# Part two's plain queries and keys behind the first quarter of w_in, and its plain values as f32 through SyncE

## The chip, the core and the metric

The kernel runs on one core of a Trainium2 chip. The metric is the time of one execution on the device in microseconds (us), from the first to the last instruction of the core; lower is better. All times below are of this one core.

## What is computed

Attention over 8 batches, 8 heads, 576 positions and 64 columns, then a feed-forward network on its output. Four heads ("plain") look at the last 32 positions, four ("dilated") at every fourth position of the last 128. All inputs and the output are f32.

```python
scores = scale * np.matmul(q, k.transpose(0, 1, 3, 2))
mask_plain = (rel >= 0) & (rel < window)                                            # window 32
mask_dil = (rel >= 0) & (rel < window * dilation) & (rel % dilation == 0)           # dilation 4
attn = softmax(np.where(masks, scores, -1e9))
x = (attn @ v).transpose(0, 2, 1, 3).reshape(B * S, H * D)                          # 4608 x 512
h = np.maximum(x @ w_in, 0.0)                                                       # w_in 512 x 2048
out = h * h @ w_out                                                                 # w_out 2048 x 512
```

## The kernel before

Heads are worked in pairs e: 0 and 1 are the plain pairs, 2 and 3 the dilated ones. A pair fills the 128 partitions, 64 rows of `sides` for each head. For batches 0 and 1 the positions are cut in two parts: part 0 has positions 0 to 255, part 1 has 256 to 575. The attention output goes, transposed, into the ring xT, and the feed-forward network takes it in token tiles: four tiles of 256 tokens at the start, then tiles of 512. A tile has a first stage (L676: w_in times xT into PSUM, then ScalarE's Relu, L687, and VectorE's square, L688, into h2T) and a second (L711: h2T times w_out, then ScalarE's copy, L718, and SyncE's store, L650). The kernel cuts this into groups of matmuls, and between the groups it puts pieces of the next batches' attention.

The order is written out by hand in the string PROGRAM (L21). What stands before its first bar runs first, what stands behind bar n runs after group n. The scheduler is off (`manual_schedule`), so each engine takes its instructions in exactly this order, and waits for what they need. The codes:

- `Lb:...` are loads of batch b. `q001` loads q and k of part 0, pairs 0 and 1 (`load_qk`, L161, one load each for q and k); `q023`, `q101`, `q123` are the like for other parts and pairs. `v0d` and `v1d` load the dilated values (L184), `v1r` the last 64 positions of these (L197), `v1p` the plain values of part 1: four loads (L178), one for each of four heads. `i0` to `i3` load the quarters of w_in (L776), `o0` to `o3` those of w_out (L781). All of these are issued by GpSimd, whose loads turn f32 into bf16 in flight.
- For batch 0: `T` transposes q and k on TensorE (L505), `C` copies the result out of PSUM (L512 to L520; a trailing `a` puts the copy on ScalarE, `v` on VectorE), `B` writes the mask as a bias, `S` are the scores (L557), `E` the exponential (L565, and for part 1 the mask product on VectorE, L568), `P` is probabilities times values (L595), `D` their sums by a matrix of ones (L611), `L` and `X` are logarithm and exponential on ScalarE, which give the reciprocal of the sums (L618, L621), `M` multiplies into xT (L628). The two digits are pair and part.
- `wN` and `WN` are N matmuls of zeros (`turn`, L475) that keep TensorE going; `W2+31` adds them onto the scores of pair 3, part 1.
- `h` casts the plain values of part 0 from a buffer of f32 into vbd, the layout that P takes (L803). This buffer, `plain`, is one of the three output buffers osb, borrowed at the start; SyncE and ScalarE load it (L745, two loads each).
- `u`, `m` build masks, `z`, `y`, `n` clear buffers; codes such as `1q1` are steps of later batches.

GpSimd's loads use eight semaphores in turn, so load number n is issued only once load n - 8 has landed. The profile shows this as a wait of GpSimd for a DMA.

The groups of the first two tiles are in an order of their own (L836): groups 0 and 1 are stage one of tile 0 for the first quarter of w_in, pairs 0, 1 and pairs 2, 3 of xT; groups 2 and 3 take the second quarter; group 4 begins tile 1 with the first quarter and pairs 2, 3; groups 5 and 6 take the third quarter for tile 0; group 7 ends what group 4 began, with pairs 0, 1; then come the rest of stage one of tile 1 and the fourth quarter.

Of the kernel before, what the change touches and what calls it, by code (L numbers as in the profile page):

```python
# [18 lines left out]


PROGRAM = (  # L21
    "L0:q001 L0:q023 L0:q101 L0:q123 L0:v0d L0:i0 L0:v1dr L0:i1 L0:v1p L0:i2 L0:i3 L0:o0 L0:o1 L0:o2 L0:o3 "
    "L1:q00123 z y L1:v0dp L1:q10123 L1:v1dpr w9 T00 C00a T10 C10a B00 B10 W2 S00 E00 B20 W1 S10 E10 u B30 W3 "
    "T20q W6 T20k C20v T30 C30v h W3 S20 E20 W2 S30 E30 T01 C01v T11 C11a P00 P10 D00 D10 L00 T21 C21v T31 "
    "C31v W4 S01 S11 X00 M00 E01 E11 P20 P30 D20 D30 L20 X20 M20 S21 S31 W2+31 E21 E31 | | P21 P31 D21 D31 L21 "
    "X21 M21 L31 X31 M31 | | P01 P11 D01 D11 L01 X01 M01 L11 X11 M11 | | | | | | | | | | | | | m n | | | | | "
    "L2:q00123 L2:q10123 | 1q1 1q3 | 1q2f 1k2f | 1k1a 1v3 | 1a2 | 1v2 1k0a 1q0v | 1o2 | 1a0 1a1 | 1k3 1o0 1o1f "
    "| 1a3 1Q0 | 1K0 1o3 | 1Q1 1K1 | 1Q2 | 1b0 | | 1Q3 1K2 L2:vwpdr L3:q00123 L3:q10123 | L2:x | | 2q0 | | 2k0 "
    "1V2 | 1b2 1p0 | 1b1 1V3 1K3 | | 1p2 1p1f | 2a0 1b3 | 2k1l 2o0 1p3f 2b0 2k1h | 2q1 2k2 L3:x | | 2q2 2p0 "
# [34 lines left out]
def kernel(  # L64
# [9 lines left out]
    nc = tc.nc  # L74
    P = nc.NUM_PARTITIONS
    B, H, S, D = q.shape
    DM, DFF = moe_w_in.shape
    NTOK = B * S
    assert H * D == DM
    bf16 = mybir.dt.bfloat16  # L80
    f32 = mybir.dt.float32
# [5 lines left out]
    NB = S // 64  # L87
# [5 lines left out]
    NT = 512  # L93
# [39 lines left out]
    xT = const.tile([P, KT, RING], bf16, name="xT")  # L133
# [345 lines left out]
    def first_step(code: str):  # L479
# [82 lines left out]
        elif what == "E":  # L562
            ps = first.pop(("S", e, part))
            to = pts[e][:, c : c + ps.shape[1]]
            nc.scalar.activation(to, ps, ACT.Exp, scale=SCALE)  # L565
            if part:
                mask = (mask_d if dil else mask_p)[:, c : c + ps.shape[1]]
                nc.vector.tensor_tensor(out=to, in0=to, in1=mask, op=ALU.mult)  # L568
        elif what == "P":
            if ("P", *pair) not in first:  # L570
                if pair in ((2, 0), (2, 1), (0, 1)):
                    od = ps_o.tile([P, 512], f32, name="po"), ps_d.tile([P, 512], f32, name="pd")
                else:
                    pool, nm = (ps_a, "pa") if part else (ps_f, "pf")
                    od = [pool.tile([P, 512], f32, name=nm) for _ in range(2)]
                first.pop("W", None)
                first["P", *pair] = od
            o, d = [x[:, y0 : y0 + w] for x in first["P", *pair]]
            o3, d3 = byr(o), byr(d)
            pt = pts[e]  # L580
            bl = blocks(0, e, part)
            y, dms = c, []
            for x, (i, r, q0, q1) in enumerate(bl):
                z = (q1 - q0) * (RES if r is None else 1)
                quads = dil and i < 8
                for rows in sides if quads else [slice(0, P)]:
                    if r is None:
                        to, rhs = o3[rows, :, q0 - m0 : q1 - m0], byr(pt[rows, y : y + z])
                    else:
                        to, rhs = o3[rows, r, q0 - m0 : q1 - m0], pt[rows, y : y + z]  # L590
                    if quads:
                        lhs = vds[0][rows, e - NE // 2, i // RES, D * (i % RES) : D * (i % RES) + D]
                    else:
                        lhs = vbd[0][:, e, i, :]
                    nc.tensor.matmul(  # L595
                        to, lhs, rhs, start=(x == 0 and y0 == 0), stop=(x == len(bl) - 1), skip_group_check=True
                    )
                if not dil:
                    dms.append((d3[:, :, q0 - m0 : q1 - m0], byr(pt[:, y : y + z])))
                y += z  # L600
            if dil and part == 0:
                dms.append((d, pt[:, 0:w]))
            elif dil:
                main = byr(pt[:, c : c + 448])
                dms += [(d3, main[:, :, 32:112]), (d3[:, :, 0:32], main[:, :, 0:32]),
                        (d3[:, :, 64:80], byr(pt[:, c + 448 : c + 512]))]
            first["D", e, part] = dms
        elif what == "D":
            dms = first.pop(("D", e, part))
            for x, (dd, rh) in enumerate(dms):  # L610
                nc.tensor.matmul(  # L611
                    dd, ones, rh, start=(x == 0 and y0 == 0), stop=(x == len(dms) - 1), skip_group_check=True
                )
        else:
            n = 512 if part == 0 else w
            if what == "L":
                first["X", e, part] = rec = r_pool.tile([P, 512], f32, name="rec")
                nc.scalar.activation(rec[:, 0:n], first["P", e, part][1][:, 0:n], ACT.Ln)  # L618
            elif what == "X":
                rec = first["X", e, part][:, 0:n]  # L620
                nc.scalar.activation(rec, rec, ACT.Exp, scale=-1.0)  # L621
            else:
                o, rec = first["P", e, part][0][:, 0:n], first.pop(("X", e, part))[:, 0:n]
                to = xT[:, e, RES * m0 : RES * m0 + n]
                if part == 0:
                    to = xT[:, e : e + 2, 0:w]
                    o, rec = [x.rearrange("p (e n) -> p e n", e=2) for x in (o, rec)]
                nc.vector.tensor_tensor(out=to, in0=o, in1=rec, op=ALU.mult)  # L628
# [24 lines left out]
    def ffn_groups(tk0: int, nt: int):  # L653
# [49 lines left out]
        def g2(m, part):  # L703
            last = tk0 + P * (m + 1) == NTOK
            if part == 0 or last and part == 2:
                cur[m] = ps_f.tile([P, DM], f32, name="pf")

            c0, c1 = (DM // 2 * (part // 2), DM // 2 * (part // 2 + 1)) if last else (0, DM)
            f0, f1 = (NF // 2 * (part % 2), NF // 2 * (part % 2 + 1)) if last else (4 * part, 4 * part + 4)
            for f in range(f0, f1):  # L710
                nc.tensor.matmul(  # L711
                    cur[m][:, c0:c1], h2[:, f, P * m : P * m + P], w_out_sb[:, f, c0:c1],
                    start=(f == 0), stop=(f == NF - 1),
                )
            if f1 == NF:
                osb = osb_pool.tile([P, DM], f32, name="osb")
                mid = (c0 + c1) // 2 if last else c1
                nc.scalar.copy(osb[:, c0:mid], cur[m][:, c0:mid])  # L718
                if last:
                    nc.vector.tensor_copy(osb[:, mid:c1], cur[m][:, mid:c1])  # L720
                for x in (c0, DM // 2) if c1 - c0 == DM and tk0 == NTOK - NT else (c0,):
                    store(osb, tk0 + P * m, x, DM // 2 if x < min(c1, DM // 2) and tk0 == NTOK - NT else c1)

        return [lambda i=i: g1(i) for i in range(NF // per)] + [
            lambda m=m, part=part: g2(m, part) for m in range(nt // P) for part in range(4)
# [17 lines left out]
    for e, engine in enumerate((nc.sync, nc.scalar)):  # L743
        for hl, rows in enumerate(sides):
            engine.dma_start(  # L745
                plain[rows, e, :, :], v[0, 2 * e + hl, 0:256, :].rearrange("(i p) d -> p i d", p=64)
            )
    near = mk[:, 0:96].rearrange("p (r m) -> p r m", r=RES)

    def put(dst, src):  # L750
        nc.scalar.copy(dst, src)
# [39 lines left out]
    def run(code):  # L791
        if code == "y":
            for nm in "qk":
                nc.gpsimd.memset(staged(1, nm)[64:80, 0, :, :], 0.0)
                nc.gpsimd.memset(staged(2, nm)[64:80, 0, 0 : H // 2, :], 0.0)
        elif code == "z":
            nc.gpsimd.memset(vbd[1][0:64, :, :, 64:128], 0.0)
            nc.gpsimd.memset(vbd[1][64:128, :, :, 0:64], 0.0)
        elif code in "mu":
            masks(int(code == "u"))  # L800
        elif code == "h":
            for rows in sides:
                nc.vector.tensor_copy(vbd[0][rows, 0:2, 0:4, rows], plain[rows, :, :, :])  # L803
        elif code == "n":
            zero_halves(kbd)
            zero_halves(vbd[0][:, NE // 2 :, 0:8, :])
        elif code[0] in "wW":
            n, _, at = code[1:].partition("+")
            turn(int(n), 512 if code[0] == "w" else 256, [int(x) for x in at])
        elif code[0] in "TCBSEPDXM" or code[0] == "L" and code[2:3] != ":":  # L810
            first_step(code)
        elif code[0] != "L":
            step(int(code[0]), code[1:])
        else:
            b, what, part, which = int(code[1]), code[3], code[4:5], code[5:]
            if what == "q":
                load_qk(b, None if part == "w" else int(part), [int(e) for e in which])
            elif what == "x":
                cross_all(b)
            elif what == "v":  # L820
                load_v(b, [0, 1] if part == "w" else [int(part)], which)
            else:
                (load_w_in if what == "i" else load_w_out)(int(part))
# [67 lines left out]
```

The softmax here doesn't subtract the row's maximum and nothing guards it: scores larger than these inputs give would overflow.

## Time and profile before

The median of three runs is 309.02 us (308.62 to 309.26). The profiled execution spans 309.7 us.

| engine | busy, us | share | instructions |
|---|---|---|---|
| TensorE, matmuls (PE) | 301.4 | 97% | 2562 |
| TensorE, weight loads (PEld) | 186.6 | 60% | 2562 |
| VectorE (DVE) | 196.2 | 63% | 645 |
| ScalarE (ACT) | 198.2 | 64% | 425 |
| GpSimd (POOL) | 93.8 | 30% | 138 |

| stretch, us | what runs | PE busy | DMA moved, GB/s |
|---|---|---|---|
| 0 to 10 | batch 0, part 0 | 8.61 of 10.00 | 122 |
| 10 to 18 | batch 0, parts 0 and 1 | 6.58 of 8.00 | 195 |
| 18 to 26.34 | groups 0 to 4, part 1 | 7.15 of 8.34 | 152 |
| 26.34 to 36 | groups 5 on, stage one | 9.66 of 9.66 | 218 |
| 36 to 53 | stage two, batch 1 | 17.00 of 17.00 | 166 |
| 53 to 79 | batches 1 and 2 | 25.32 of 26.00 | 171 |

The granted TensorE clock is 0.998 of full speed. How to read it: PE's busy time takes in the time that matmuls stand in its pipeline, so a busy PE is not PE at its peak; a gap in it is a true wait, though. The DMA view gives bytes as they are written, so a GpSimd load counts half of what it reads. A landing is the issue's start plus the time "to landing". The DMA queues have the names q0 (GpSimd), q1 (SyncE) and q10 (ScalarE); in this program a packet is one row of a load.

### The profile page before, as it was taken

How to read it: one execution, taken by the hardware profiler on the slowest of the kernel's cores; microseconds unless marked ns; L12 is line 12 of the kernel's file. 1: busy time of each engine (PE TensorE's matmuls, PEld its weight loads, DVE VectorE, ACT ScalarE, POOL GpSimd, SP SyncE). 2: the span in 40 equal slices, each digit the busy share in tenths (PEclk: the TensorE clock that was granted, in tenths of full speed). 3: DMA queues.
4: the chain of work that ended last, by engine and by line, in shares of the span. 5: the costliest groups of instructions: out<-in, count | busy, mean ns of one | idle time of the engine just before them, and what ended most of it. 6: DMA issues, size and time to landing. Idle time of an engine off the chain costs nothing.

```text
span 309.7 us, 6806 instructions
## 1 busy us (share of the span) xinstructions
PE 301.4 (97%) x2562; PEld 186.6 (60%) x2562; DVE 196.2 (63%) x645; ACT 198.2 (64%) x425; POOL 93.8 (30%) x138
## 2 busy tenths in 40 slices
PE   8898999999999999999999999999999999999995
PEld 3578856958855555555599555555555555445544
DVE  1555567888989889975798469946994334104400
ACT  7576748849977967795388547854686456216511
POOL 8489775546317345501551041000000000000000
PEclk9999999999999999999999999999999999999999
DMA  7999999999999979999799976502200210121022
GB/s 103 195 143 212 208 151 172 175 141 186 171 130 174 165 139 182 185 144 155 109 127 134 154 121 93 103 8 61 68 3 0 70 69 0 35 69 34 0 61 77
DMA packets 80288, 35.05 MB, mean 113 GB/s; under 512 B 49920, under 2 KB 75648, under 8 KB 80256
## 3 DMA queue, kind: packets, MB, share of 16 engines
q0 software_dynamic: 46592, 18.23, 52.4%
q1 hardware_dynamic: 32976, 16.06, 28.2%
q10 hardware_dynamic: 688, 0.33, 0.5%
q8 instruction: 20, 0.33, 0.4%
q14 instruction: 12, 0.10, 0.1%
HBM read 36.90 MB, written 9.44 MB: 150 GB/s over the span
## 4 chain that ended last, share of the span: by engine, by line
PE 81%; DMA 9%; ACT 3%; POOL 3%; issue 1%; DVE 1%; POOLq 0%; ACTq 0%
PE pf L711 38%; PE pf L676 35%; DMA w_in<-in_moe_w_in_dram 6%; DMA kb<-in_k_dram 4%; PE po L421 3%; PE pd L423 2%; PE pa L312 2%; PE pa L318 1%; POOL qb L161 1%; ACT h2T L687 1%; POOL kb L161 1%; PE pa L236 1%; ACT pt L322 1%; ACT qT L256 1%; ACT rec L425 0%
## 5 line engine op out<-in xcount | busy, mean ns | idle before, releaser
L676 PE MATMUL pf<-xT,w_in 128*128 128x256 bf16 (+1 forms) x768 | 133.5, 326 | 1.3 <-DMA w_in<-in_moe_w_in_dram 1.2
L711 PE MATMUL pf<-w_out_sb,h2T 128*128 128x512 bf16 (+1 forms) x592 | 134.2, 373 | 0.0
L676 PEld LDWEIGHTS <-w_in 128*128 128x128 bf16 x768 | 82.2, 114 | 36.6 <-DMA w_in<-in_moe_w_in_dram 1.8
L687 ACT ACTIVATE h2T<-pf 128x512 bf16<-128x512 f32 x144 | 83.8, 599 | 25.5 <-PE pf L676 24.8
L711 PEld LDWEIGHTS <-h2T 128*128 128x128 bf16 x592 | 54.3, 98 | 53.5
L688 DVE TENSOR_TENSOR h2T<-h2T 128x512 bf16<-128x512 bf16 x144 | 57.9, 422 | 40.2 <-ACT h2T L687 39.0
L718 ACT COPY osb<-pf 128x512 f32<-128x512 f32 (+1 forms) x37 | 21.0, 566 | 43.8 <-PE pf L711 35.8
L436 DVE TENSOR_TENSOR xT<-po,rec 128x288 bf16<-128x288 f32 (+2 forms) x51 | 23.2, 454 | 30.9 <-ACT rec L426 30.4
L178 POOL DMA_DIRECT2D vbd<-in_v_dram x36 | 25.7, 735 | 42.0 <-PE pd L423 37.2
L425 ACT ACTIVATE rec<-pd 128x288 f32<-128x288 f32 (+2 forms) x51 | 20.9, 411 | 20.4 <-PE pd L423 20.4
L322 ACT ACTIVATE pt<-pa 128x352 bf16<-128x352 f32 (+6 forms) x56 | 27.6, 499 | 7.1 <-PE pa L312 4.2
L426 ACT ACTIVATE rec<-rec 128x288 f32<-128x288 f32 (+2 forms) x56 | 24.8, 444 | 1.8
L421 PEld LDWEIGHTS <-vbd 128*128 128x128 bf16 x286 | 17.1, 97 | 9.4 <-issue 0.4
L256 DVE COPY qT<-xx 64x288 bf16<-64x288 bf16 x84 | 21.3, 253 | 1.1
L191 POOL DMA_DIRECT2D vd<-in_v_dram x24 | 14.7, 627 | 17.2 <-DMA kb<-in_k_dram 9.1
L161 POOL DMA_DIRECT2D qb<-in_q_dram x18 | 13.0, 720 | 16.7 <-DMA xx<-qb 15.1
L421 PE MATMUL po<-pt,vbd 128*128 128x32 bf16 (+3 forms) x256 | 17.5, 198 | 0.0
L260 DVE COPY kbd<-xx 64x288 bf16<-64x288 bf16 x36 | 17.0, 471 | 0.5
L423 PE MATMUL pd<-pt,mk 128*128 128x32 bf16 (+6 forms) x138 | 15.5, 203 | 0.0
L197 POOL DMA_DIRECT2D vbd<-in_v_dram x16 | 9.6, 602 | 14.6 <-PE pd L423 5.1
L161 POOL DMA_DIRECT2D kb<-in_k_dram x18 | 12.8, 711 | 0.8 <-DMA kb<-in_k_dram 0.5
L312 PE MATMUL pa<-qT,kbd 128*128 128x96 bf16 (+2 forms) x144 | 12.2, 202 | 0.0
(99 smaller groups left out, 240.3 us busy)
## 6 DMA issues: line engine op xcount, KB each, us to landing
out_dram<-osb SPq DMA_DIRECT2D x18, 128.0 KB, 3.4
qb<-in_q_dram POOLq DMA_DIRECT2D x7, 320.0 KB, 8.1
kb<-in_k_dram POOLq DMA_DIRECT2D x7, 320.0 KB, 10.4
vd<-in_v_dram POOLq DMA_DIRECT2D x32, 64.0 KB, 7.5
w_in<-in_moe_w_in_dram POOLq DMA_DIRECT2D x4, 512.0 KB, 8.0
w_out_sb<-in_moe_w_out_dram POOLq DMA_DIRECT2D x4, 512.0 KB, 13.0
qb<-in_q_dram POOLq DMA_DIRECT2D x7, 256.0 KB, 7.3
kb<-in_k_dram POOLq DMA_DIRECT2D x7, 256.0 KB, 8.1
```

The costliest lines, as they stand in the source:

```text
L161: nc.gpsimd.dma_start(t[0:n, part, hs, :], src[b, hs, t0 : t0 + RES * n, :].rearrange("h (p r) d -> p h (r d)", r=RES))
L178: nc.gpsimd.dma_start(dst[rows, e, i0:i1, rows], v[b, 2 * e + hl, 64 * i0 : 64 * i1, :].rearrange("(i p) d -> p i d", p=64),)
L256: copy(qT[rows, e, :, m0 : m0 + n].rearrange("p (c j) m -> p j c m", j=2)[:, jj, :, :], src)
L322: nc.scalar.activation(pt[:, off : off + n], ps[:, 0:n], ACT.Exp, scale=SCALE)
L421: nc.tensor.matmul(oo, vb[:, e, i, :], rh, start=(x == 0), stop=(x == len(mms) - 1), skip_group_check=True)
L423: nc.tensor.matmul(dd, ones[:, :], rh, start=(x == 0), stop=(x == len(dms) - 1), skip_group_check=True)
L426: nc.scalar.activation(rec[:, 0:n], rec[:, 0:n], ACT.Exp, scale=-1.0)
L436: nc.vector.tensor_tensor(out=tok, in0=o if o is o3 else o[:, 0:n], in1=rec if o is o3 else rec[:, 0:n], op=ALU.mult)
L676: nc.tensor.matmul(acc[u][:, nt * x + y0 : nt * x + y1], w_in_sb[piece][:, kt, c0 : c0 + 509 : 4], xT[:, kt, t0 : t0 + y1 - y0], start=(kt ...
L687: nc.scalar.activation(hv, acc[u][:, :].rearrange("p (x n) -> p x n", x=per), ACT.Relu)
L688: nc.vector.tensor_tensor(out=hv, in0=hv, in1=hv, op=ALU.mult)
L711: nc.tensor.matmul(cur[m][:, c0:c1], h2[:, f, P * m : P * m + P], w_out_sb[:, f, c0:c1], start=(f == 0), stop=(f == NF - 1),)
```

## The change

It does four things. Part one of the loads: `q101`, part 1's q and k of the plain pairs, is issued behind `i0`, the first quarter of w_in, and not ahead of it. Second, `v1p`, the four GpSimd loads of part 1's plain values, is gone. In its place, step `t` takes two output buffers, writes one column in each from xT (which holds the loads back until pairs 0 and 1 of part 0 are in xT), and has SyncE load the values as f32, two loads for each buffer; the steps `H0` and `H1` cast them into vbd on VectorE, two casts for each pair. Third, PROGRAM is put in an order that fits: the dilated pairs of part 1 are transposed and scored first, the plain ones after group 1; the plain probabilities times values (P01, P11) come after group 4, not group 3, and P11 after the whole of pair 0. One big copy (C31) moves to ScalarE, `W2+31` becomes `W5+31`, the idle `W4` goes, and the PSUM buffers of one P are other ones. Fourth, the stores of the two blocks ahead of the last tile are cut in two halves of columns.

The aim is that w_in's quarters stand further ahead in GpSimd's queue, and that four small loads leave it.

```diff
-    "L0:q001 L0:q023 L0:q101 L0:q123 L0:v0d L0:i0 L0:v1dr L0:i1 L0:v1p L0:i2 L0:i3 L0:o0 L0:o1 L0:o2 L0:o3 "
-    "L1:q00123 z y L1:v0dp L1:q10123 L1:v1dpr w9 T00 C00a T10 C10a B00 B10 W2 S00 E00 B20 W1 S10 E10 u B30 W3 "
-    "T20q W6 T20k C20v T30 C30v h W3 S20 E20 W2 S30 E30 T01 C01v T11 C11a P00 P10 D00 D10 L00 T21 C21v T31 "
-    "C31v W4 S01 S11 X00 M00 E01 E11 P20 P30 D20 D30 L20 X20 M20 S21 S31 W2+31 E21 E31 | | P21 P31 D21 D31 L21 "
-    "X21 M21 L31 X31 M31 | | P01 P11 D01 D11 L01 X01 M01 L11 X11 M11 | | | | | | | | | | | | | m n | | | | | "
+    "L0:q001 L0:q023 L0:q123 L0:v0d L0:i0 L0:q101 L0:v1dr L0:i1 L0:i2 L0:i3 L0:o0 L0:o1 L0:o2 L0:o3 L1:q00123 "
+    "z y L1:v0dp L1:q10123 L1:v1dpr w9 T00 C00a T10 C10a B00 B10 W2 S00 E00 B20 W1 S10 E10 u B30 W3 T20q W6 "
+    "T20k C20v T30 C30v h W3 S20 E20 W2 S30 E30 T21 C21v T31 C31a P00 P10 D00 D10 L00 X00 P20 P30 D20 D30 L20 "
+    "X20 M00 t S21 S31 W5+31 M20 E21 E31 | | T01 C01v T11 C11a P21 P31 D21 D31 S01 S11 L21 X21 M21 L31 X31 M31 "
+    "E01 H0 H1 E11 | | | P01 D01 L01 X01 M01 P11 D11 L11 X11 M11 | | | | | | | | | | | | m n | | | | | "
...
-                    pool, nm = (ps_a, "pa") if part else (ps_f, "pf")
+                    pool, nm = (ps_a, "pa") if pair == (1, 1) else (ps_f, "pf")
...
-                for x in (c0, DM // 2) if c1 - c0 == DM and tk0 == NTOK - NT else (c0,):
-                    store(osb, tk0 + P * m, x, DM // 2 if x < min(c1, DM // 2) and tk0 == NTOK - NT else c1)
+                for x in (c0, DM // 2) if c1 - c0 == DM and tk0 + P * m >= NTOK - NT - 256 else (c0,):
+                    store(osb, tk0 + P * m, x, DM // 2 if x < min(c1, DM // 2) and tk0 + P * m >= NTOK - NT - 256 else c1)
...
+    late = {}
...
+        elif code == "t":
+            for e in range(2):
+                late[e] = osb_pool.tile([P, DM], f32, name="osb")[:, 0:320].rearrange("p (i d) -> p i d", d=D)
+                nc.vector.tensor_copy(late[e][:, 0, 0:1], xT[:, e, 0:1])
+                for hl, rows in enumerate(sides):
+                    nc.sync.dma_start(
+                        late[e][rows, :, :], v[0, 2 * e + hl, 256:S, :].rearrange("(i p) d -> p i d", p=64)
+                    )
+        elif code in ("H0", "H1"):
+            e = int(code[1])
+            for rows in sides:
+                nc.vector.tensor_copy(vbd[0][rows, e, 4:NB, rows], late[e][rows, :, :])
```

## The prediction

> **What bounds the kernel now.** I read the critical chain first, then the waits of TensorE, then the rows of the first 27 us, then the DMA view in short stretches. Two rows of the waits say where TensorE stood still for data once the FFN had begun (us in total, times, longest):
>
> ```profile
> PE pf L676 <- DMA w_in<-in_moe_w_in_dram: 1.2, 1, 1.2
> PE pa L236 <- DMA kb<-in_k_dram: 0.6, 1, 0.6
> ```
>
> The chain of the start, in order of time (start us, us, what), names the first of the two:
>
> ```profile
> 7.47 10.45 DMA w_in<-in_moe_w_in_dram
> 17.91 0.28 issue
> 18.20 1.30 POOL vbd L178 x2
> 19.50 6.79 DMA w_in<-in_moe_w_in_dram
> 26.29 0.05 issue
> 26.34 3.68 PE pf L676 x32
> ```
>
> The third quarter of w_in is issued at 19.50, behind the four plain value loads of part two (L178), and lands at 26.29. From 26.34 TensorE has no gap: the table by stage gives it 9.66 of 9.66 us (26.34 to 36) and 17.00 of 17.00 us (36 to 53). Its next gap is the 0.6 us at 64.1, where batch 2's keys land, issued at 53.03 and 11.02 us on the way in the chain. After that it is TensorE at 97% to the end. So only two moments count: when the dense stretch starts (26.34 now), and whether the keys at 64.05 then hold it up. A start that is x later costs x less the 0.6 us; one that is earlier gains only as far as those keys come earlier too.
>
> **What the skill says.** (1) The Trainium skill, "DMA: Bandwidth & Descriptors", section "Queues, rings and completion order": each DMA engine takes turns between the queues that have work, a packet at a time. The trace agrees. In 9.5 to 10.5 us both kinds were loaded, GpSimd's q/k rows of 512 B (q0) and SyncE's f32 value rows of 256 B (q1, a few left on q10):
>
> ```profile
> q0 software_dynamic: 264, 0.13, 95.1%
> q1 hardware_dynamic: 208, 0.05, 38.7%
> q10 hardware_dynamic: 27, 0.01, 3.2%
> ```
>
> 264 against 235 packets in one us is nearly one for one. (2) Same page, section "Issuing engines are not separate DMA queues": another issuing engine saves the issuer's time, not DMA time. What the trace gives for that is below. (3) Same page, section "SWDGE vs HWDGE vs iDMA": a cast in flight needs GpSimd's queue, which is why the change needs VectorE for the cast.
>
> **The change part by part.** *GpSimd's queue.* Part two's plain q and k (L161, 80x4 rows of 512 B each) go behind w_in's first quarter. The order of what stands before the second quarter changes, its sum doesn't: first quarter earlier, second as before (13.95 + 7.4 = 21.35). By landings in the DMA view the third quarter came at 26.29 (19.50 + 6.8) and the fourth at 28.9 (20.27 + 8.6), 2.6 us for a quarter; from the second to the third it was 4.94, so the four value loads cost 4.94 - 2.6 = 2.3 us of queue. That is what leaves GpSimd's queue.
>
> *What comes back on SyncE's queue.* Four loads of 64 x 5 rows of 256 B: 1280 packets, 80 for each of 16 engines. Price of one: in 11 to 12 us 395 packets of 512 B went alone, 16/395 = 40 ns per packet and engine; in 9.5 to 10.5 each engine did 16.5 of those (668 ns) and 14.7 of SyncE's, so 332/14.7 = 23 ns each. 80 x 23 = 1.8 us of every engine. The saving in DMA time is 2.3 - 1.8 = 0.5 us, no more.
>
> *When they land.* The loads wait for a marker copy that reads xT after L628 of heads 0 and 1. In the trace:
>
> ```profile
> 14.07 0.63 ACT L621 ACTIVATE rec<-rec 128x512 f32<-128x512 f32 x1
> 15.26 0.69 DVE L628 TENSOR_TENSOR xT<-pf,rec 128x512 bf16<-128x512 f32 x1
> ```
>
> Its input is ready at 14.70; VectorE is late because two L514 copies stand before it, and the new order has them done earlier (one of the big copies goes to ScalarE). So L628 ends near 14.7 + 0.69 = 15.4, two marker copies at about 0.15 (the like of it at L742 takes 169 ns) end at 15.7. SyncE issued two such loads in 1.66 us (3.35 to 5.01), so four take 3.3, from 15.7 to 19.0. The first packet came 2 us after issue on ScalarE's queue (issued 3.36, first one in the stretch 4.9 to 5.5) and over 3 us on SyncE's (none by 6.6): first data at 17.7 to 18.8. By then the queue it shares holds 1 KB rows of w_in, quarter after quarter, which go at 16 x 2 us / 408 = 78 ns in the stretch 23 to 25:
>
> ```profile
> q0 software_dynamic: 408, 0.40, 123.5%
> ```
>
> One for one, a value packet waits for a w_in packet: 78 + 23 = 101 ns, and 80 of them take 8.1 us, 17.7 to 25.8. From the last packets (some 7 after 11.0) to the landing of SyncE's second load at 11.8 it was 0.8 to 0.9 us. Last load landed: 26.7. At the short end packets go as in 9.5 to 10.5 (63 ns): 17.7 + 5.0 + 0.8 = 23.5. At the long end first data is at 18.8 and a w_in packet takes 98: 18.8 + 80 x 0.121 + 0.9 = 29.4. I take 26.7, since w_in is what stands there.
>
> *The new wait.* VectorE casts in its order: first head pair 0, then pair 1, then the mask of pair 1 (L568), then P11 on TensorE can run. L803 took 0.42 us for 512 columns, so 0.26 to 0.3 for 320: 26.7 + 0.3 = 27.0. L568: 0.87 for two, 0.45: 27.45. P11 and D11: the four groups P01, P11, D01, D11 ran from 23.21 to 24.11, so half, 0.45: 27.9. Behind P11 on TensorE stands the whole dense stretch. Behind the casts on VectorE stand two L688 squares, for second-stage work that starts near 36, and L628 of heads 0 and 1; these matmuls have two other groups (2 x 0.87 us) ahead, so I cost them nothing. The dense stretch starts at 27.9 instead of 26.34: +1.55.
>
> *The second quarter.* L676 took it at 21.44, just landed at 21.35. With value packets between, about 70 of the 80 before it on the slowest engines, it lands up to 70 x 23 ns = 1.6 us later, 22.95. Then three groups (2.6), P01 and D01 (0.45) end at 26.0: hidden behind the wait for P11. But it means that quick value loads don't start the dense stretch much before 26.4.
>
> *What costs nothing.* 2.3 us of GpSimd issue (L178, 1.35 + 1.32 with waits): GpSimd has slack, its loads wait for landings. The copy moved to ScalarE: about 0.7 us in the gap of 0.30 and 1.21 around 12.7. P-tiles in other PSUM buffers, three more idle matmuls (0.11 us each): TensorE waits there for w_in. Stores of the last but one tile in halves: SyncE waits there for ScalarE's copies, 36.9 us at the longest.
>
> *Sum.* +1.55 at the start, less the 0.6 us at 64.1, which then falls away (the keys come 0.5 us earlier or the same): +0.95. 309.02 + 0.95 = 310.0 us.
>
> **Rivals.** *No change.* SyncE's packets flow faster than one for one, the values are there by 24.5, and the second quarter's delay sets the start: 26.0 + 0.45 = 26.45, or 26.3. The keys still land near 64: 309.0 us. For: the second quarter was taken as it landed. Against: one for one in the only second that shows both.
> *Faster.* The second quarter isn't delayed much, the third lands at 21.35 + 2.6 plus a part of 1.8, 24.0 to 25.3, and the start is at 25.2 (-1.1). Of this the keys let through the 0.5 us of saved DMA time and up to 0.6 of their own slack if output stores at 42 to 45 no longer delay batch 1's keys: 308.2 us. For: DMA engines were part idle at 20 to 22 (523 packets of small size in 2 us), which the new order fills. Against: landings follow the slowest engine, and the second quarter's stragglers were still landing at 21.35.
> *Much slower.* The long end, 29.4: + 0.3 + 0.45 + 0.45 = 30.6, +4.2, less 0.6: 312.6 us. For: w_out's 4 KB rows stand behind w_in.
>
> **How the numbers follow.** Chances: forecast 0.5, much slower 0.1, no change 0.2, faster 0.2. The first is not higher since first data and the pace beside 1 KB rows are nowhere shown together. Faster by over 0.2% means below 308.4: the faster rival and a little of the others, 0.22. Slower means above 309.64: forecast and much slower, less the forecast's low edge, 0.57. The rest, 0.21. Range: 308.3 to 312.0. It leaves out a good half of the faster rival (0.12, with its centre at 308.2) and the upper half and more of the much slower one (0.08 with its tail).
>
> **What would show it.** Right: SyncE's value loads take 8 us or more to land; VectorE waits for that DMA at the new casts; L676's dense run starts after P11, near 27.9, and the 0.6 us wait at L236 is gone. Wrong: values landed by 24.5 (packet price), the wait at L676 for w_in still the last one before the dense run (no change), a dense run before 25.5 with the keys landing before 63.5 (faster).

## The result, and the profile after

The change made the kernel slower: 318.16 us in the median of four executions, against 308.88 us (308.62 to 309.26) before. The ratio is 1.0278, with a 95% interval of 1.021 to 1.0346. (One of the four, of 327.06 us, fell in a slower state and is not in the ratio; the other three took 316.16, 316.97 and 319.35 us, 317.5 in the mean.) So the time rose by 8.6 us in the mean. The forecast was 310.0 us, in a range of 308.3 to 312.0: the side was right, the size was not.

The waits of TensorE after the change (us in total, times, longest):

```profile
PE pa L595 <- DVE pt L568: 4.2, 1, 4.2
PE pf L676 <- DMA w_in<-in_moe_w_in_dram: 0.6, 1, 0.6
```

The wait of 1.2 us for w_in's third quarter is gone (the 0.6 us here are for the second quarter, at 21.67), and the 0.6 us for the keys of batch 2 (L236) is no longer in the list. In their place stands one wait of 4.2 us, for the masked probabilities of pair 1, part 1 (L568). L568 isn't slow; it stands behind the casts on VectorE, and those wait for SyncE's loads. VectorE's waits in the first 60 us have this row:

```profile
DVE vbd L813 <- DMA osb<-in_v_dram: 4.2, 3, 1.7
```

The chain of the start, in order of time (start us, us, what), runs through the same places:

```profile
17.44 11.05 DMA osb<-in_v_dram
28.49 0.02 issue
28.51 0.04 DVE vbd L813
...
29.02 0.42 DVE pt L568
29.45 0.04 issue
29.49 0.56 PE pa L595 x6
30.05 0.40 PE pa L611 x6
30.45 11.33 PE pf L676 x88
```

The last value load is issued at 17.44 and lands 11.05 us later, at 28.49. The cast, the mask, P11 and D11 follow without a gap, and then the dense stretch. VectorE's timeline shows what stands at both ends of the loads (start us, us, engine, line, operation, and in brackets the idle time before it):

```profile
14.56 0.69 DVE L628 TENSOR_TENSOR xT<-pf,rec 128x512 bf16<-128x512 f32 x1 [1.07 <-ACT rec L621]
...
26.29 0.48 DVE L813 CAST vbd<-osb 64x320 bf16<-64x320 f32 x1 [1.67 <-DMA osb<-in_v_dram]
28.51 0.48 DVE L813 CAST vbd<-osb 64x320 bf16<-64x320 f32 x1 [1.74 <-DMA osb<-in_v_dram]
29.02 0.41 DVE L568 TENSOR_TENSOR pt<-pt,mask_p 128x480 bf16<-128x480 bf16 x1
```

The loads could start from 15.25, when L628 was done, and TensorE's timeline shows what comes of their landing:

```profile
29.49 0.56 PE L595 MATMUL pa<-pt,vbd 128*128 128x32 bf16 x6 [4.21 <-DVE pt L568]
29.86 0.59 PE L611 MATMUL pa<-pt,mk 128*128 128x32 bf16 x6
30.26 11.52 PE L676 MATMUL pf<-xT,w_in 128*128 128x256 bf16 x88
41.62 6.21 PE L711 MATMUL pf<-w_out_sb,h2T 128*128 128x512 bf16 x27
```

The same rows of the kernel before:

```profile
26.34 9.80 PE L676 MATMUL pf<-xT,w_in 128*128 128x256 bf16 x88 [1.19 <-DMA w_in<-in_moe_w_in_dram]
35.97 6.21 PE L711 MATMUL pf<-w_out_sb,h2T 128*128 128x512 bf16 x28
```

The dense run of 88 matmuls of L676 begins at 30.26, 3.92 us later than before. It also takes longer: 11.52 us, where the same 88 took 9.80 us before. The table by stage says why (stretch, us, busy us of PE, PEld, DVE, ACT and POOL with their instructions, then the granted TensorE clock, the DMA share and GB/s):

```profile
30.26:33.85 3.59, 3.59 (x20) 2.48 (x18) 1.16 (x3) 1.51 (x3) 3.59 (x6) 0.50 1.07 215
33.85:41.60 7.75, 7.75 (x73) 7.73 (x71) 3.87 (x10) 5.76 (x10) 2.99 (x5) 1.00 1.16 143
```

For its first 3.59 us the dense run has half the clock (0.50). Only 17 of the 88 matmuls start in it (the other 3 of the 20 in this row are of L611), against some 33 at the pace of the 71 that start in the next 7.75 us. So the second stage (L711) starts at 41.62, where it was 35.97: +5.65, which is 3.92 + 1.72 but for rounding. At the end of the span +5.5 is left of it (315.2 against 309.7 us): the 0.6 us at L236 came back, and about as much was lost again later, which I did not attribute.

The traces differ by 5.5 us and the times by 8.6. The rest comes from which executions were profiled: that of before took 311.46 us, 2.6 above its median, and that of after 316.97, 0.5 below its mean. 5.5 + 2.6 + 0.5 = 8.6.

### The profile page after: what moved, and what is told of

The parts are those of the page before. It is cut to its first block, busy times and chain, and to the rows that moved or that the text cites. A ratio compares the mean times of both kernels' runs of the same rounds, so it can differ in the third digit from the quotient of the medians.

```text
span 315.2 us, 6798 instructions
## 1 busy us (share of the span) xinstructions
PE 302.1 (96%) x2529; PEld 188.2 (60%) x2561; DVE 198.0 (63%) x650; ACT 199.3 (63%) x426; POOL 91.2 (29%) x134
## 4 chain that ended last, share of the span: by engine, by line
PE 85%; DMA 6%; ACT 3%; DVE 2%; issue 2%; POOL 1%; SPq 0%; ACTq 0%; POOLq 0%
PE pf L711 37%; PE pf L676 36%; DMA osb<-in_v_dram 4%; PE po L421 3%; DMA kb<-in_k_dram 2%; PE pd L423 2%; PE pa L312 2%; PE pa L318 1%; PE pa L236 1%; ACT h2T L687 1%; POOL qb L161 1%; ACT pt L322 1%; ACT qT L256 0%; ACT rec L425 0%; POOL kb L161 0%
## 5 line engine op out<-in xcount | busy, mean ns | idle before, releaser
L676 PE MATMUL pf<-xT,w_in 128*128 128x256 bf16 (+1 forms) x758 | 133.7, 329 | 1.3 <-DMA w_in<-in_moe_w_in_dram 0.6
L711 PE MATMUL pf<-w_out_sb,h2T 128*128 128x512 bf16 (+1 forms) x570 | 131.0, 373 | 1.2
L676 PEld LDWEIGHTS <-w_in 128*128 128x128 bf16 x768 | 82.9, 114 | 36.8 <-DMA w_in<-in_moe_w_in_dram 1.1
L711 PEld LDWEIGHTS <-h2T 128*128 128x128 bf16 x592 | 54.3, 98 | 53.5
L178 POOL DMA_DIRECT2D vbd<-in_v_dram x32 | 23.0, 740 | 58.1 <-PE pd L423 51.2
L256 DVE COPY qT<-xx 64x288 bf16<-64x288 bf16 x84 | 20.3, 241 | 1.1
L260 DVE COPY kbd<-xx 64x288 bf16<-64x288 bf16 x36 | 16.9, 470 | 0.5
L197 POOL DMA_DIRECT2D vbd<-in_v_dram x16 | 9.7, 617 | 8.6 <-PE pd L423 7.2
## 6 DMA issues: line engine op xcount, KB each, us to landing
w_out_sb<-in_moe_w_out_dram POOLq DMA_DIRECT2D x4, 512.0 KB, 15.7
```

The lines of the kernel that those rows point to most:

```text
L178: nc.gpsimd.dma_start(dst[rows, e, i0:i1, rows], v[b, 2 * e + hl, 64 * i0 : 64 * i1, :].rearrange("(i p) d -> p i d", p=64),)
L676: nc.tensor.matmul(acc[u][:, nt * x + y0 : nt * x + y1], w_in_sb[piece][:, kt, c0 : c0 + 509 : 4], xT[:, kt, t0 : t0 + y1 - y0], start=(kt ...
L711: nc.tensor.matmul(cur[m][:, c0:c1], h2[:, f, P * m : P * m + P], w_out_sb[:, f, c0:c1], start=(f == 0), stop=(f == NF - 1),)
```

## Experiments

My first theory was that all of the loss lies in SyncE's four loads: their short rows take turns with GpSimd's rows, first with w_in's, then with w_out's long ones, so that they land late; the wait then idles TensorE, and the idle time halves its clock. The rivals were that the new order of PROGRAM or of GpSimd's loads costs time too, that the slow clock comes from something else than the idle time, and that starting the loads earlier would cure it. Each group of runs had its own executions of the kernel before, with medians of 310.08 us (e1 to e4), 309.85 (e5 to e8) and 309.18 (r1 to r3).

**e2: the kernel after, with the value loads back on GpSimd.** All else of the change stays.

```diff
-    ... L0:v1dr L0:i1 L0:i2 L0:i3 ...
+    ... L0:v1dr L0:i1 L0:v1p L0:i2 L0:i3 ...
-    "X20 M00 t S21 ...  E01 H0 H1 E11 ...
+    "X20 M00 S21 ...    E01 E11 ...
```

> The changed kernel with its plain values of part two loaded by GpSimd again, behind the second quarter of w_in as before the change; no f32 loads by SyncE, no casts. All the rest of the change stays: late q and k of the plain pairs, the new order, the stores in halves. Theory A: the whole loss is the SyncE loads, so no wait of TensorE for VectorE at P11, dense stretch from 26.3 or a little earlier, 308.3 to 309.3 us. Rival (the later q and k and the new order cost a part of it): 311 us or more.

Measured: 309.01 us in the median, ratio 0.9975 (0.9959 to 0.9991). The wait at P11 is gone, and TensorE's timeline gives:

```profile
24.51 10.01 PE L676 MATMUL pf<-xT,w_in 128*128 128x256 bf16 x88
34.35 6.21 PE L711 MATMUL pf<-w_out_sb,h2T 128*128 128x512 bf16 x28
```

On GpSimd's queue the four loads were issued from 15.78 on and landed at 20.92 to 21.41; on SyncE's queue the last one landed at 28.49. So the four loads and their casts are the whole loss. The new order, the copy on ScalarE, the other PSUM buffers and the halved stores together cost nothing, as the prediction had them.

**e3: the kernel before, with the value loads alone moved to SyncE.** The reverse of e2.

```diff
-    ... L0:i1 L0:v1p L0:i2 ...  X00 M00 E01 ...  | P01 P11 D01 D11 ...
+    ... L0:i1 L0:i2 ...         X00 M00 t E01 ...  | H0 H1 P01 P11 D01 D11 ...
```

> The kernel before with only the values' part of the change: the four GpSimd loads gone, f32 loads by SyncE held back until L628 of pairs 0 and 1, casts by VectorE ahead of P01. Queue order of q and k and the order of the steps as before. Theory A: the last values land at 28 to 30, TensorE waits for the casts at P01, dense stretch from 30 to 31.5, 314 to 318 us. Rival (the order matters as much): 309 to 311 us.

Measured: 325.7 us, ratio 1.0515 (1.0483 to 1.0548), worse than the whole change and beyond the 314 to 318 us that I had expected. TensorE's waits and VectorE's last cast:

```profile
PE pa L595 <- DVE vbd L813: 10.9, 1, 10.9
```

```profile
36.95 0.48 DVE L813 CAST vbd<-osb 64x320 bf16<-64x320 f32 x1 [5.60 <-DMA osb<-in_v_dram]
```

The casts began at 24.85, 25.61, 30.87 and 36.95. SyncE issued its loads from 15.81, nearly as in the kernel after, but its first packets came only in 19 to 20, and GpSimd issued w_out from 16.83, 1.2 us earlier. So more of the value rows met w_out's long rows. The DMA view of 28 to 29 us (packets, MB, share of 16 engines):

```profile
q0 software_dynamic: 55, 0.20, 97.0%
q1 hardware_dynamic: 55, 0.01, 9.8%
```

55 against 55: one row for one row, whatever their lengths. The stretches of 1 us from 26, 27, 29, 30 and 31 give 63 and 65, 59 and 57, 49 and 49, 57 and 57, 54 and 54. A GpSimd row is some 3.7 KB in the mean here (0.20 MB by 55), and each of the 16 engines moves one of SyncE's 256 B rows in 16 / 55 = 0.29 us, where the prediction had 0.10 beside w_in's rows.

**e4: the kernel after, with w_out issued later.** GpSimd's memsets `z` and `y` stand ahead of w_out's loads, which then start at 26.56 and not at 18.03.

```diff
-    ... L0:i2 L0:i3 L0:o0 L0:o1 L0:o2 L0:o3 L1:q00123 z y L1:v0dp ...
+    ... L0:i2 L0:i3 z y L0:o0 L0:o1 L0:o2 L0:o3 L1:q00123 L1:v0dp ...
```

> The changed kernel with GpSimd's memsets of steps z and y (8 us or more of its time) moved ahead of the loads of w_out, which so start near 27 and not at 18. Theory A (a SyncE packet waits for one GpSimd packet of whatever size, and the last tenth of the values had to wait beside 4 KB rows of w_out): the four value loads land by about 25.5 instead of 28.4 and the wait at P11 shrinks from 4.2 to under 1.5 us; L711 then waits for w_out, so the time in all says nothing. Rival (SyncE's queue has a pace of its own): last landing near 28.4 again.

Measured: 313.3 us in a single execution, 3.7 below the profiled one of the kernel after (316.97; the others took 316.16 and 319.35), so the size is no more than indicated. The last cast starts at 25.85, where it was 28.51. TensorE's timeline:

```profile
26.82 0.56 PE L595 MATMUL pa<-pt,vbd 128*128 128x32 bf16 x6 [2.95 <-DVE pt L568]
27.59 10.99 PE L676 MATMUL pf<-xT,w_in 128*128 128x256 bf16 x88
```

In the kernel after, 92% of SyncE's packets had gone by 24.0 (1240 of 1344, see below), but the last few took until 28; here all but 10 had gone by 25.0. So w_out's long rows are what draws the end out. Two expectations failed: the wait of TensorE was still 2.95 us and not under 1.5, since cast and mask follow the landing anyway, and w_out came late without making L711 wait. The clock still fell for 3.41 us, and the 88 matmuls took 10.99 us. This version is still slower than the kernel before.

**e1 and e5: the kernel after, with idle matmuls in the gap ahead of P11.** They keep TensorE busy while it waits for the values, and write a PSUM tile that P11 starts anew. If the idle time halves the clock, they give the full clock back.

```diff
-    ... P01 D01 L01 X01 M01 P11 D11 ...
+    ... P01 D01 L01 X01 M01 F36 P11 D11 ...      (e1; F64 in e5)
+        elif code[0] == "F":
+            first["P", 1, 1] = od = [ps_a.tile([P, 512], f32, name="pa") for _ in range(2)]
+            for _ in range(int(code[1:])):
+                nc.tensor.matmul(od[0][:, 0:256], idle[:, 0:P], idle[:, :], start=True, stop=True, skip_group_check=True)
```

> The changed kernel with 36 idle matmuls of 256 columns put on TensorE ahead of P11, where it waited 4.2 us; nothing else. Theory A (two costs: the values' landing, and a TensorE clock that fell to half speed for 6.8 us from 27.0 on, because TensorE had stood idle): the clock stays at full speed, the run of 88 matmuls of L676 takes 9.8 us as before the change and not 11.5, P11 still starts near 29.5, the time falls by 1.7 to 2.5 us to about 314. Rival (the clock fell for another reason, or that run was slow for lack of data): no change, 316 to 319, and a spell at half speed again.

> The changed kernel with 64 idle matmuls ahead of P11, not 36, so that TensorE is busy from 24.3 to about 31.3 and past the last landing. Theory A (standing idle is what halved the clock): no spell at half speed before the end of the run, the 88 matmuls of L676 take 9.8 to 10.0 us (11.5 in the changed kernel, 11.1 with 36), the dense stretch starts near 31.7, and the time is 314 to 315 although the start is later than the changed kernel's 30.3. Rival: a spell at half speed all the same, 317 us or more.

e1 measured 318.62 us, ratio 1.0215 (1.0122 to 1.0309). In its trace the values landed at 30.35, later than the fill reached (28.4): TensorE still stood for 2.95 us, the clock fell for 3.41 us, and the 88 matmuls took 11.10 us. By itself it decides nothing; one of its executions, of 314.31 us, had a mean clock of 1.000.

e5, with 64 of them, measured 316.96 us (316.76 and 317.16), ratio 1.0234 (1.015 to 1.0317), with a mean clock of 0.999 in both executions. TensorE's timeline:

```profile
24.38 7.15 PE L817 MATMUL pa<-idle 128*128 128x256 bf16 x64
31.37 0.39 PE L595 MATMUL pa<-pt,vbd 128*128 128x32 bf16 x6
...
31.82 9.78 PE L676 MATMUL pf<-xT,w_in 128*128 128x256 bf16 x88
```

No idle time, no half clock: the 88 matmuls take 9.78 us again, and P11 takes 0.39 us in place of 0.56. Against the trace of after, the dense run starts 1.56 us later (31.82) and the second stage still starts a little earlier (41.43 against 41.62). The time didn't fall, since the fill itself ends at 31.4 and gives back by its length what it gains by the clock. The start (near 31.7) and the length of the run (9.8 to 10.0 us) were as expected, but the expected 314 to 315 us didn't follow from them: they put the second stage where the kernel after had it.

**e8: e2, with a pause of VectorE.** The values come by GpSimd as in e2, and two rounds of needless memsets (`n n`) stand on VectorE where H0 and H1 stood. No SyncE load is left; TensorE is idle all the same.

```diff
-    "X31 M31 E01 E11 | | | P01 ...      (e2)
+    "X31 M31 E01 n n E11 | | | P01 ...
```

> The kernel of e2, but VectorE clears two buffers twice (6.2 us of memsets, step n) ahead of the mask of pair 1, so that TensorE stands idle ahead of P11 with no SyncE load anywhere. Theory A (idle time alone halves the clock afterwards): P11 some 5 us later than e2's 24.06, a spell at half speed of 6 to 7 us, the 88 matmuls of L676 take 11 us or more, and the time is e2's plus 6 to 7 us, 315 to 316. Rival (the clock has to do with the transfers): full speed, 314 us or less.

Measured: 318.2 us (316.97 and 319.43), ratio 1.0274 (1.0178 to 1.0369). TensorE's timeline, and the table by stage for 29 to 34 us:

```profile
31.86 0.63 PE L595 MATMUL pa<-pt,vbd 128*128 128x32 bf16 x6 [6.94 <-DVE pt L568]
...
32.70 11.63 PE L676 MATMUL pf<-xT,w_in 128*128 128x256 bf16 x88
```

```profile
29.00:34.00 5.00, 2.14 (x19) 1.70 (x19) 3.57 (x8) 0.91 (x2) 5.00 (x5) 0.57 1.06 212
```

After 6.94 us of idle time the clock is 0.57 in the mean of this stretch, and the 88 matmuls take 11.63 us. So the idle time alone halves the clock, whatever caused it; with e5, which takes the idle time away and leaves the loads, this settles that rival. The pause was longer than meant: P11 starts 7.8 us later than in e2 (31.86 against 24.06) and not some 5, and the time is above the expected 315 to 316 us. This trace also has an earlier half-clock spell, of 3.41 us from 12.63, which the pause didn't make.

**e6: the kernel after, with the loads at the very start.** Step `t` comes first in PROGRAM, with its marker read from mk.

```diff
-    "L0:q001 L0:q023 ...   X20 M00 t S21 ...
+    "t L0:q001 L0:q023 ... X20 M00 S21 ...
-                nc.vector.tensor_copy(late[e][:, 0, 0:1], xT[:, e, 0:1])
+                nc.vector.tensor_copy(late[e][:, 0, 0:1], mk[:, 0:1])
```

> The changed kernel with the values' f32 loads issued by SyncE at the start, behind its two other value loads, with a marker copy that reads a mask constant in place of xT; the rest as changed. Theory A (a SyncE load is slow beside w_in's and w_out's long rows, and quick beside q and k's 512 B rows): all values landed by 16, no wait at P11; 80 packets of 23 ns delay q, k and the first quarter by 1.8 us, which the start mostly gets back at w_in's later quarters; dense stretch from 24.5 to 26, 308.5 to 310 us. Rival (early queries and keys are the tighter path): 310 us or more, TensorE waiting for q and k at L505.

Measured: 311.67 us (310.09 to 312.77), ratio 1.0048 (1.0028 to 1.0069). TensorE's timeline:

```profile
12.40 0.34 PE L505 MATMUL pa<-mk,kb 80*64 80x80 bf16 x8 [1.29 <-DMA kb<-in_k_dram]
...
28.22 9.77 PE L676 MATMUL pf<-xT,w_in 128*128 128x256 bf16 x88
```

The values are there in time, and P11 waits 0.86 us. But now the short rows take turns with the first q and k: TensorE waits 1.29 us for keys at 12.40, and the clock is halved early, for 6.83 us from 12.6. The rival held: the cost moves to the front, most of it is saved, and some 1.5 us stay. The early half clock isn't the whole of these: 12 of the 20 executions have a mean clock of 0.998 or more, and they took 310.1 to 312.0 us. I had expected 308.5 to 310 us.

**e7: e2, with q101 ahead of w_in's first quarter again.** What remains of the change is the order of PROGRAM and the halved stores.

```diff
-    "L0:q001 L0:q023 L0:q123 L0:v0d L0:i0 L0:q101 L0:v1dr ...      (e2)
+    "L0:q001 L0:q023 L0:q123 L0:q101 L0:v0d L0:i0 L0:v1dr ...
```

> The kernel of e2 (values by GpSimd) with q and k of the plain pairs ahead of the first quarter again, so only the new order of the steps and the halved stores are left of the change. Theory A: the dense stretch starts at 24.5 in e2 because w_in's third quarter no longer waits for value loads that wait for landings; with the first quarter late again it starts at 25.5 to 26.4, 309 us or no different from before. Rival (the order alone brings it): 24.5 again and the same time as e2.

Measured: 309.98 us (309.34 to 311.87), ratio 1.0018 (0.999 to 1.0045): no difference. In its trace the 88 matmuls begin at 24.74, only 0.23 us after e2's, as the rival had it (I had expected 25.5 to 26.4). So moving q101 behind w_in brings little on its own either.

**r1, r2, r3: the kernel before, the kernel after, and e2 again.**

> The kernel before, unchanged, profiled once more. The profiled executions of the two kernels differ by 5.5 us, their medians by 9.3. Theory A (the wait and the slow clock explain what the traces show, and the rest is that the first profiled execution of the kernel before was 2.6 us longer than its median): this execution's dense stretch starts earlier than 26.34, near 24.5 to 25.5, and the span is 306.5 to 308. Rival (it is typical, and the rest is lost in executions of the changed kernel that no trace shows): 26.3 and 309.7 again.

> The changed kernel, unchanged, profiled once more. Theory A: the last landing of the values depends on how far w_in had come when they were issued, so it moves by a us or two from one execution to the next: last landing 27.5 to 31, the wait at P11 4 to 7 us, one spell at half speed, 316 to 319 us. Rival (fixed costs): 28.4 and 4.2 us again.

> The kernel of e2 once more with more rounds, since its gain over the kernel before is of the size of the scatter. Theory A (the dense stretch starts earlier by 1 us or more, and nothing after it takes that back): ratio to the kernel before 0.995 to 0.998. Rival: no difference, 0.999 to 1.001, as for the order of the steps alone.

r1 measured 309.3 us, ratio 1.0012 (0.9985 to 1.0039). In its trace, of 308.4 us, the wait for w_in's third quarter is gone and L676 runs without a gap from 24.90, but TensorE waits for keys earlier (0.86 us at 12.14, 0.36 at 14.19), the clock is halved for 3.41 us from 14.58, and L711 starts at 35.61, not much earlier than 35.97. So the start differs between executions of the same kernel. r3 measured 309.11 us (308.75 to 311.04), ratio 1.0001 (0.9987 to 1.0015): the 0.25% of e2 were not repeated, so there is no version here that surely beats the kernel before. r2 measured 320.95 us (320.21 and 321.7), ratio 1.0376 (1.0336 to 1.0416), more than the first time and than the expected 316 to 319. Its trace shows why, in VectorE's last cast and TensorE's wait:

```profile
33.13 0.48 DVE L813 CAST vbd<-osb 64x320 bf16<-64x320 f32 x1 [5.28 <-DMA osb<-in_v_dram]
```

```profile
34.11 0.56 PE L595 MATMUL pa<-pt,vbd 128*128 128x32 bf16 x6 [8.56 <-DVE pt L568]
```

and in the DMA view of 28 to 29 us:

```profile
q0 software_dynamic: 58, 0.20, 99.8%
q1 hardware_dynamic: 31, 0.01, 5.6%
```

The same kernel, its loads issued at nearly the same time (15.3, against 15.5), landed its last one at 33.1 and not at 28.5. SyncE's queue has 1344 packets in all (1280 rows, and 64 of 4 bytes that I take for four completions on 16 engines). Six traces, by the DMA view in stretches of 1 us:

| trace | packets in 18 to 19 | left at 24.0 | w_out issued from | last cast starts |
|---|---|---|---|---|
| e4 | 345 (and 298 in the next us) | 148 | 26.56 | 25.85 |
| after | 510 | 104 | 18.03 | 28.51 |
| e5 | 192 | 341 | 17.48 | 28.98 |
| e1 | 243 | 360 | 16.86 | 30.37 |
| r2 | 151 | 429 | 16.78 | 33.13 |
| e3 | none | 733 | 16.83 | 36.95 |

In the first 1 or 2 us SyncE's rows sometimes get ahead of one for one, by very different amounts. From then on it is one for one, mostly at 127 to 163 a us beside w_in's rows and 49 to 65 beside w_out's. What is left when w_out's rows come, from about 24 to 25 us, goes at the slow pace: the more is left at 24.0, the later is the last cast. With w_out held back (e4), 148 left at 24.0 were there by 25.8; with it, 104 took until 28.5. In the traces with more left, w_out was also issued up to 1.25 us earlier; only e4 moves it by itself.

The clock against the idle time ahead of the dense run (the half-clock spells by the clock record of the trace; r1, r3 and e7 have no idle time and no spell there, like e2):

| trace | TensorE idle, us | half clock from, us | for, us | 88 matmuls of L676, us |
|---|---|---|---|---|
| before | 1.19 | none | 0 | 9.80 |
| e5 | none | none | 0 | 9.78 |
| e6 | 0.86 | none here | 0 | 9.77 |
| e2 | none | none | 0 | 10.01 |
| e4 | 2.95 | 26.68 | 3.41 | 10.99 |
| e1 | 2.95 | 31.42 | 3.41 | 11.10 |
| after | 4.21 | 27.0 | 6.83 | 11.52 |
| e8 | 6.94 | 29.7 | 6.83 | 11.63 |
| r2 | 8.56 | 29.37 | 10.24 | 12.08 |
| e3 | 10.95 | 27.23 | 13.65 | 11.73 (for 96) |

All spells of the table last a whole number of times 3.41 us. In the kernel after, the fall at 27.03 came 1.75 us into the wait, which began at 25.28, and the clock rose again only at 33.86. The length of one wait doesn't decide alone: in the first 20 us, where TensorE's work has many small gaps, the clock fell in r1, e8 and e6 (at 14.58, 12.63 and 12.59, for 3.41, 3.41 and 6.83 us) after waits of at most 0.86, 0.64 and 1.29 us, and in e7 it stayed full after one of 1.93 us.

## Why the prediction was right, and where it was wrong

**What sets the time: right.** The prediction said that only the start of the dense stretch and the wait at 64.1 count. From the first L711 matmul to the end of the span it is 273.7 us before and 273.6 after, and 272.7 to 273.8 in all thirteen traces, although the start of L711 differs by over 16 us between them (33.96 in r3, 50.22 in e3).

**GpSimd's queue: right in direction, but the change didn't need the loads to leave.** The third quarter of w_in landed at 24.95 and not at 26.29, and the second at 21.62, within the predicted 21.35 to 22.95. The gain was hidden behind the wait for P11. With the order of before, taking the four loads off the queue shows such a gain too (24.43 in e3). But with the new order and the four loads back on GpSimd, the third quarter landed still earlier: at 24.27 in e2, 23.98 in r3 and 23.71 in e7. So in the changed kernel the predicted 2.3 us of queue are not seen as a gain.

**When the loads start: right.** L628 ended at 15.25 (predicted 15.4), SyncE issued from 15.46 to 18.05 (predicted 15.7 to 19.0), and the first packets came in 17 to 18 (predicted 17.7 to 18.8).

**When they land: this is the step that failed first.** "One for one, a value packet waits for a w_in packet: 78 + 23 = 101 ns, and 80 of them take 8.1 us ... Last load landed: 26.7." The pace was nearly right: 127 to 153 packets a us in 19 to 24, 141 in the mean, are 16 / 141 = 113 ns. What failed is "I take 26.7, since w_in is what stands there." W_in doesn't stand there to the end. From 24 to 25 on it is w_out's rows, and with them a pair takes 16 / 55 = 0.29 us. In the kernel after, 1240 of 1344 packets had gone by 24.0, ahead of my schedule, thanks to the 510 in one us; then SyncE moved 59, 22, 13 and 10 packets a us. By an estimate from the 55 that all 16 engines moved in a us of e3, 10 to 13 are the work of 3 or 4 engines: the others were done, and the last load landed with these. I had the fact (the "much slower" rival names w_out's 4 KB rows) and gave it a chance of a tenth. I also took a mean pace over 16 engines for the time of the last one, although I had written in another place that landings follow the slowest engine. Measured: 28.49, and 28.96, 30.35 and 33.11 in three other traces with the same loads (e5, e1, r2). This is +1.8 us in the first trace and up to +6.4. That it was not more in the first one is luck: SyncE's early 510 packets are the most of all these traces.

**Cast, mask, P11 and D11: mis-sized a little.** A cast took 0.48 us, not 0.26 to 0.3; I had scaled L803's 0.42 us by its columns, but a cast of 320 columns took longer than one of 512. The mask took 0.41 (predicted 0.45). P11 and D11 took 0.77 us to the start of L676, not 0.45, since they ran at the halved clock. Together +0.5. From 27.9 to 30.26 it is 2.36 us: 1.8 from the landing, the rest from these.

**A term left out: the clock.** I priced a longer wait of TensorE as its own length. The Trainium skill, "TensorE: Matmul & The Clock Gate", "Part 1: The HAM clock gate", says that TensorE falls to half its clock after an idle window of about 3.4 us and gets it back after a busy one. The runs agree on the spells (3.41, 6.83, 10.24 and 13.65 us), but not on the idle window: in the kernel after the clock fell 1.75 us into the wait. The spell reached 3.59 us into the dense run. It cost 11.52 - 9.80 = 1.7 us there, and made the 0.3 us at P11 and D11 (0.77 us at half the clock, 0.45 in e2 at the full one). e8 makes it without the loads, and e5 takes it away with the loads. The forecast itself had TensorE stand for 1.45 us only (26.0 to 27.45). No trace has such a wait at this place (0.86 us in e6 and 1.19 before left the clock full, 2.95 in e4 and e1 did not), so the term comes in with the late landing as far as the runs show. But the "much slower" rival had it stand for over 4 us, and gave that no price beyond its length. Its dense start of 30.6 was met within 0.4 us, and still the trace lost 5.5 us and not 3.6: most of the difference is the clock's 1.72.

**The 0.6 us at 64.1: gone, but not by the change alone.** The keys landed at 60.95 and not at 64.05, and the wait is gone as forecast. In r1, the kernel before unchanged, it is gone as well (keys at 62.21). So it is not a fixed part of the kernel's time, and taking it off the median of 309.02 us was not sound.

**What costs nothing: right.** e2 and r3 have all of those edits and show no loss (0.9975 and 1.0001).

The sum in the trace: +3.92 for the start (predicted +1.55), +1.72 for the clock (predicted 0), and -0.1 for the rest (predicted -0.6; about 0.5 went elsewhere): +5.5 in place of +0.95. What is beyond that in the times, 3.1 us, is which executions were profiled.

**What stays open.** The traces of e2, e7 and r3 start L711 at 34.35, 34.58 and 33.96, those of the kernel before at 35.97 and 35.61. That is 1.0 to 2.0 us earlier, and no median shows it. The profiled executions of before were slower than most of its timed ones (311.46 and 310.16, against medians of 308.88 and 309.3), so its traces probably show starts later than usual. An estimate: a time is 1.8 us more than its span (311.46 and 309.7), and from L711 on it is some 273.3 us, so an execution of 308.88 us starts L711 near 33.8, like r3. No trace of such an execution is there to show it. Nor do the runs show why SyncE's rows get ahead at first by such different amounts, or which engines lag.

## What to carry to other kernels

In these runs, many short rows on one queue beside long rows on another moved one for one, at the pace of the long ones. So time such a load by what the other queue holds until the last row has gone, and by the slowest engine. If TensorE is to wait for 3 us or more, add the cost of its clock: 1.2 to 2.3 us here (e4, r2), on top of the wait; a shorter wait may cost it too. And moving a load to another queue doesn't move it to other DMA engines: on GpSimd's queue these four loads took their turn ahead of w_in's third quarter and landed by 21.41 (e2), on SyncE's they took turns row by row with w_in and w_out, and the last one landed at 28.49.

## What was not expected of the hardware

- Two queues take turns row by row, not by larger units: 55 and 55, 49 and 49, 57 and 57, 54 and 54 packets a us beside rows of some 3.7 KB (e3). In stretches of 0.3 us, about the time of one such pair, the mean over 26 to 32 us is 16.9 and 16.9, one of each for each of the 16 engines, with a scatter of 2 to 3. The Trainium skill, "DMA: Bandwidth & Descriptors", "Queues, rings and completion order", speaks of 9 to 17 descriptors that are drained from one queue before the switch; no such thing shows in these loads, where the trace's packets are single rows.
- At its start SyncE's queue moved 510 packets in one us, while GpSimd's did 112; in other traces of such loads it was 345, 243, 192, 151 and none.
- The clock fell 1.75 us into a wait (after), 2.81 us into one (e4), and stayed full after waits of 1.19 us (before) and 1.93 us (e7). A wait of 2.95 us was followed by a spell of 3.41 us (e1, e4).
- A cast of 64x320 from f32 to bf16 took 0.48 us (L813), one of 64x512 took 0.42 us (L803). The Trainium skill, "VectorE: DVE Perf Modes", "What auto-detection actually checks", has a possible reason: for f32 into bf16 VectorE doubles its pace only if the outermost dimensions of input and output are both even or equal. The output of L813 is 5 blocks of 64; its input is written as 5 blocks too, but lies in one run of 320, and which of the two counts is not known. L803 has 8 blocks. No run here varied this.
